# Three rooms for the summed weights, and a second room for g, in a block attention and squared-ReLU feed-forward kernel

## The chip, the cores and the metric

The kernel runs on one core of a Trainium2 chip. The metric is the device time of one execution in microseconds (us). The kernel before took 905.09 us (median of 3 runs, 904.5 to 905.71). One further execution was profiled; it took 905.52 us, of which 903.5 us lie between its first and its last instruction (the span). All rows below are from that execution.

## The reference

q, k and v have shape (8, 8, 576, 64): batch, heads, sequence, head width. Attention runs inside chunks of 64 positions only. The result is laid out as 4608 tokens of width 512 and goes through a feed-forward layer with a squared ReLU.

```python
scores = scale * np.matmul(q_c, k_c.transpose(0, 1, 2, 4, 3))   # chunks of 64
scores = scores - np.max(scores, axis=-1, keepdims=True)
attn = np.exp(scores)
attn = attn / (np.sum(attn, axis=-1, keepdims=True) + 1e-09)
out = np.matmul(attn, v_c)
...
h = x @ w_in            # 512 -> 2048, weights arrive as float64
r = np.maximum(h, 0.0)
g = r * r
return (g @ w_out).astype(np.float32)
```

## The kernel before

**Tiling.** The tokens are 36 pairs of chunks (128 tokens each), in 7 blocks: three of 4 pairs, four of 6. The hidden width 2048 is 16 slices of 128. Every float32 operand of the large products is split in a high and a low part, and each product takes three matmuls (high·high, high·low, low·high).

**Direct passes.** The first three blocks run slice by slice: 12 matmuls into h (L604), ReLU, square and split on ScalarE and VectorE, and two slices later 12 matmuls into the accumulators o (L640). These are 48 slices.

**Mixed blocks.** The last four blocks compute h with one level of a fast 2×2 scheme: 7 block products instead of 8. A *unit* (class Mixed) is one pair of hidden slices of one block: 7 products of 6 matmuls (L691) from mixed weights (the ring, 10 rooms, fetched from a scratch tensor in DRAM by L681) and mixed tokens (xc, made by build, L1225 and L1227). There are 8 units a block, 32 in all. Products accumulate in two PSUM banks, A (side 0) and C (side 1). Between products, ScalarE takes copies (keep, L697) and VectorE adds (add, L700) into float32 rooms: kept(0) for the first slice of the pair (gf0), kept(1) for the second (gf1). Then both are squared (L706) and split (high L709 on ScalarE, low L713 on VectorE): slice 0 into gs_s, slice 1 into gs_f. The second matrix product of a unit (L723, 6 groups with gs_f, then 6 with gs_s) stands behind the 7 products of the next unit. The third product needs bank A's copy, the fourth restarts bank C and so needs the unit's first add.

**Weight sums.** Four of the seven mixed weights of a slice pair are sums (s1 to s4). mix_weights makes them in three temp rooms on VectorE (L754 to L771). put then casts one (L774, ScalarE), subtracts for the low part (L778, VectorE) into the tile combo, and stores it to DRAM (L781, issued by GpSimd); a cast waits until the store before it has left combo. The other three weights are copied as they are (L790). There are 8 slice pairs, so 32 puts. They run beside the direct passes; the slots of wi12 to wi15 are taken over by xc and gs_f of the mixed blocks.

**Attention.** The pairs from 8 on (class Quad) run in clumps of 64 small matmuls on TensorE (L345 for the pair before, L298 for this one), with tiles e and p in two rooms each.

**Order.** Plan lists every step with a cost, the tiles it reads and writes, and a rank (lower goes first). Plan.run walks through a time line of its own and so fixes the order of each engine's instructions. On the chip each engine takes its instructions in that order and waits for the data of each. A gate only bars a step from being placed before another in the plan; it is no wait on the chip.

Of the kernel before, what the change touches and what calls it, by code (L numbers as in the profile page):

```python
# [20 lines left out]
def kernel(  # L21
# [24 lines left out]
    P = 128  # L46
# [228 lines left out]
    class Quad:  # L275
# [29 lines left out]
                nc.vector.tensor_reduce(self.m[:, c], four[c][:, 0], axis=AX.X, op=ALU.max)  # L305

        def less(self):
            self.e = late["pool"].tile([P, HH, 2, CH], F32, name=f"e{self.pair}", tag="e")
            for c in range(2):
                nc.vector.tensor_tensor(  # L310
                    self.e[:, :, c], four[c][:, 0], self.m[:, c].broadcast_to([P, HH, CH]), op=ALU.subtract
                )
# [17 lines left out]
            )  # L330

        def keep_p(self):
            self.p = late["pool"].tile([P, HH, 2, 2, CH // 2], F32, name=f"p{self.pair}", tag="p")
            nc.scalar.copy(self.p, self.et)

        def move_p(self, b, m):
# [199 lines left out]
        at = 2 * NCC * HN + i * HN  # L536
        return aside()[:, at:at + HN]

    def kept(i):

        return room(("g", i), lambda: gp.tile([P, 2 * HN], F32, name=f"gf{i}", tag=f"g{i + 1}", bufs=1))

    def in_slot(f, name, shape):
# [128 lines left out]
    class Mixed(Step):  # L672
# [3 lines left out]
        def __init__(self, b, p):  # L676
            self.b, self.p = b, p
            self.m = ((b - NCB) * NFP + p) * len(WAYS)

        def fetch(self, i):  # L680
            nc.gpsimd.dma_start(  # L681
# [15 lines left out]
            nc.scalar.copy(snap(i), sides[side][:, :HN])  # L697

        def add(self, i, h, side, s):
            nc.vector.tensor_tensor(kept(i)[:, h * HN:(h + 1) * HN], sides[side][:, :HN], snap(s), op=ALU.add)  # L700

        def positive(self):
            nc.scalar.activation(kept(1)[:, :HN], sides[0][:, :HN], AF.Relu)  # L703

        def square(self, i):
            nc.vector.scalar_tensor_tensor(kept(i), kept(i), 0.0, kept(i), op0=ALU.max, op1=ALU.mult)  # L706

        def high(self, i):
            nc.scalar.copy(split_g(i)[0], kept(i))  # L709

        def low(self, i):
            h, l = split_g(i)
            nc.vector.tensor_tensor(l, kept(i), h.bitcast(F32), op=ALU.subtract)  # L713

        def mm_out(self, i, j, u):
            b, p = self.b, self.p
# [14 lines left out]
    class Combos:  # L731
# [6 lines left out]
        def temp(self, i, n=1):  # L738
            return room("temp", lambda: gp.tile([P, 3, QW], F32, name="temp", tag="g2", bufs=1))[:, i:i + n]

        def out(self):
            return room("combo", lambda: wst.tile([P, 2, QW], F32R, name="combo", tag=f"a{VBUFS}"))

        def half(self, q):
# [25 lines left out]
            nc.vector.tensor_tensor(t, h, t, op=ALU.subtract)  # L770
            nc.vector.tensor_tensor(t, t, l, op=ALU.add)  # L771

        def high(self, i):
            nc.scalar.copy(self.out()[:, 0], self.temp(i)[:, 0])  # L774

        def low(self, i):
            o = self.out()
            nc.vector.tensor_tensor(o[:, 1], self.temp(i)[:, 0], o[:, 0].bitcast(F32), op=ALU.subtract)  # L778

        def store(self, name):  # L780
            nc.gpsimd.dma_start(  # L781
                out=combos[self.p, side_of[name]], in_=self.out().rearrange("p l n -> p (l n)")
            )

        def plain(self, q):
# [158 lines left out]
    def program():  # L944
# [165 lines left out]
        def scores(pair, gate):  # L1110
            x = quads[pair]
            i = pair % 2
            add(PE, 0.6, x.scores, ["qt", "kt"], ["sc", "A0", "C0"] + [("at", n) for n in range(2) if pair == NN],
                slack=SLACK, gate=gate)
            add(DVE, TWO, x.top, ["sc"], [("m", i)])
            add(DVE, TWO, x.less, ["sc", ("m", i)], [("e", i)])
            add(ACT, ONE, x.exps, [], [("e", i)])
            add(DVE, TWO + TINY, x.sums, [("e", i)], [("z", i)])
            add(DVE, TWO, x.norm, [("z", i)], [("e", i)])
            add(DVE, 0.73, x.turn_p, [("e", i)], ["et"])  # L1120
            add(ACT, ONE, x.keep_p, ["et"], [("p", i)] + [("p", i, *y) for y in itertools.product(range(2), repeat=2)])
            for b, m in itertools.product(range(2), repeat=2):
                add(SP, ISSUE, lambda b=b, m=m: x.move_p(b, m), ["et"], [("p", i, b, m)], size=P * DM // 2)

        def values(pair, gate):
            x = quads[pair]
            add(PE, 0.6, x.values, [("a", pair % VBUFS), ("p", pair % 2)] + [("p", pair % 2, *y) for y in itertools.product(range(2), repeat=2)], ["xt", "A1", "C1"], slack=SLACK, gate=gate)
# [52 lines left out]
        def wide(k):  # L1180

            return [("wh", item["i", k]), ("wl", item["i", k])]

        def mix_weights(c, gate):
            fs = [y for f in (2 * c.p, 2 * c.p + 1) for y in wide(f)]
            for q in ("a11", "a12", "a22"):
                add(POOL, 1.0, lambda q=q: c.plain(q), fs, [("combo", c.p, side_of[q])], size=P * DM * 4, gate=gate)
            T = [("temp", i) for i in range(3)]

            def put(i, name):  # L1190
                add(ACT, 0.4, lambda: c.high(i), [T[i]], ["ch"] + [("a", VBUFS)])
                add(DVE, 0.42, lambda: c.low(i), [T[i], "ch"], ["cl"])
                add(POOL, 1.0, lambda: c.store(name), ["ch", "cl"], [("combo", c.p, side_of[name])], size=P * DM * 4)

            add(DVE, 0.69, lambda: c.both_of(0, "21", "22", ALU.add), fs, T[:2], gate=gate)
            add(DVE, 0.42, lambda: c.join(0), [T[1]], [T[0]])
# [57 lines left out]
        def mixed(s, n):  # L1254
            first = s.m == 0
            rank, p.rank = p.rank, -20
            temp = [("temp", i) for i in range(3)] if first else []
            A, C = ["A0", "A1"], ["C0", "C1"]
            if n == 0:
                add(ACT, 0.5, lambda: s.keep(0, 0), A, ["s0"])  # L1260
            elif n == 1:
                add(DVE, 0.56, lambda: s.add(0, 0, 1, 0), C + ["s0"], [("kept", 0, 0)] + (["g"] if first else []))
            elif n == 2:
                add(ACT, 0.5, lambda: s.keep(1, 0), A, ["s1"])
            elif n == 3:
                add(ACT, 0.5, lambda: s.keep(0, 1), C, ["s0"])
            elif n == 4:
                add(DVE, 0.56, lambda: s.add(1, 1, 0, 0), A + ["s0"], [("kept", 1, 1)] + temp)
            elif n == 5:
                add(DVE, 0.56, lambda: s.add(0, 1, 1, 1), C + ["s1"], [("kept", 0, 1)])  # L1270
            elif n == 6:
                add(ACT, 0.5, lambda: s.positive(), A, [("kept", 1, 0)] + temp)
                square_of(s, 1)
                square_of(s, 0)
            p.rank = rank

        def square_of(s, i):
            p.rank = -1
            add(DVE, 0.95, lambda: s.square(i), [], [("kept", i, h) for h in range(2)])
            ends_to_come.append((s, i))  # L1280
            finish()

        ends_to_come = []

# [5 lines left out]
                parts_of(s, i)  # L1290
                p.rank = rank

        def parts_of(s, i):
            first = s.m == 0
            g = [("kept", i, h) for h in range(2)]
            for m, e, fn, cost in ((0, ACT, s.high, 0.82), (1, DVE, s.low, 0.95)):
                old = []
                if first:
                    old = wide(NF - 2) + wide(NF - 1) if i else [("g" + y, n) for y in "hl" for n in range(2)]
                add(e, cost, lambda fn=fn: fn(i), g + [("sg", i, 0)] * m, [("sg", i, m)] + old)  # L1300

        def mixed_group(s, i, j):
            n = item["o", 2 * s.p + i]
# [23 lines left out]
            else:  # L1327
                when.append(ends - NF + 0.3 + j * (NF - 1.3) / (SB - 1))
        mixers = [Combos(c) for c in range(NFP)]
        mix_at = [NF + 2 + (ends - NF - 9) * c / NFP for c in range(NFP)]  # L1330
        n = NF

        def clump(k, gate):
# [27 lines left out]
        for b in range(NCB, len(blocks)):  # L1361
            for c in range(NFP):
                s = Mixed(b, c)
                p.rank = 100
                fetch_ring(s)
                if c == 0:
                    p.rank = -1
                    build(b == NCB)
                p.rank = LASTS

# [6 lines left out]
                if c == 0 and b > NCB:  # L1377
                    outs(6)
                for i, more in enumerate((0, 4 if s.m == 0 else 0, 0, 0, 0, 0, 0)):
                    product(s, i)  # L1380
                    mixed(s, i)
                    if more:
                        outs(more)
                if 1 <= c <= SB and b < len(blocks) - 1:
                    at = outs(3)
                    clump(k, at)
# [2 lines left out]
                if some:  # L1389
                    outs(len(some))  # L1390
                some = [
                    (lambda s=s, i=i, j=j: mixed_group(s, i, j), i) for i in (1, 0) for j in range(blocks[b])
                ]
        outs(len(some))
        p.run()

# [33 lines left out]
```

## Time and profile before

| | |
|---|---|
| median of 3 runs | 905.09 us |
| profiled execution | 905.52 us |
| its span | 903.5 us |
| TensorE busy | 852.5 us, 94% of the span |
| VectorE, ScalarE, GpSimd busy | 548.3, 369.4, 242.4 us |
| direct passes end, mixed blocks begin | 320.15 us |
| second unit begins | 367.02 us |

TensorE is busy almost throughout. What is to be read is where in the span it is not, and what it waits for there. A row of the timeline gives the start, the duration, the engine, the line and tile, the number of instructions merged, and in brackets the idle time before it with what ended that.

### The profile page before, as it was taken

The page shows a single profiled execution, that of the slowest core. Times are in us where ns is not written, and L with a number is a line of the kernel's source. Part 1 is how long each engine was busy: PE and PEld are TensorE (multiplying, and loading weights), DVE is VectorE, ACT ScalarE, POOL GpSimd, SP SyncE. Part 2 cuts the span into 40 slices and gives each one's busy share as a digit, 9 for nine tenths or more (in the row PEclk, how much of TensorE's full clock was granted, in tenths as well). Part 3 has the DMA queues.
Part 4 walks back from the last instruction along what each step waited for, and adds up shares of the span by engine and source line. Part 5 has one row for each costly group of instructions (what it writes and reads, how often), then busy time and mean ns, then how long its engine had stood idle before and what let it go on. Part 6 is the DMA issues. An engine that isn't in the chain of part 4 may idle for free.

```text
span 903.5 us, 16529 instructions
## 1 busy us (share of the span) xinstructions
PE 852.5 (94%) x6142; PEld 732.0 (81%) x6142; DVE 548.3 (61%) x962; ACT 369.4 (41%) x669; POOL 242.4 (27%) x432
## 2 busy tenths in 40 slices
PE   9999999999999943999999999999999999999998
PEld 7787778888878832888888988888988888989896
DVE  6999994754755674555567565558555556533333
ACT  5898874444444431332224333225333324322221
POOL 2000022433551222333321423331332321313100
PEclk9999999999999976899999999999999999999999
DMA  8884525765984343567664866765766653644411
GB/s 203 256 260 135 200 48 131 155 140 119 251 172 102 90 111 99 167 148 171 157 140 101 239 141 155 167 154 116 219 151 136 149 135 82 202 113 125 121 46 70
DMA packets 241503, 132.72 MB, mean 147 GB/s; under 512 B 185744, under 2 KB 200336, under 8 KB 241424
## 3 DMA queue, kind: packets, MB, share of 16 engines
q0 software_dynamic: 47360, 80.77, 33.1%
q1 hardware_dynamic: 191808, 50.24, 25.1%
q8 instruction: 49, 0.80, 0.4%
q10 hardware_dynamic: 2256, 0.66, 0.3%
q14 instruction: 30, 0.25, 0.1%
HBM read 103.81 MB, written 24.12 MB: 142 GB/s over the span
## 4 chain that ended last, share of the span: by engine, by line
PE 79%; DVE 8%; issue 4%; DMA 3%; ACT 2%; SPq 2%; POOL 1%; DVEq 0%; POOLq 0%; ACTq 0%
PE o L723 30%; PE side L691 22%; PE o L640 12%; PE h L604 12%; PE side L345 2%; DVE gs_s L713 2%; PE side L298 2%; ACT gs_s L709 1%; SPq L260 1%; DVE gf L700 1%; ACT aside L697 1%; DMA k_raw<-in_k_dram 1%; DMA woraw<-in_moe_w_out_dram 1%; DVE woa L175 1%; DVE wia L175 1%
## 5 line engine op out<-in xcount | busy, mean ns | idle before, releaser
L691 PE MATMUL side<-xc,ring 128*128 128x384 f32 x1344 | 248.7, 340 | 42.6 <-DVE gf L700 29.5
L691 PEld LDWEIGHTS side<-xc,ring 128*128 128x128 f32 x1344 | 237.5, 190 | 51.7 <-DVE gf L700 19.8
L681 POOL DMA_DIRECT2D ring<-combos x224 | 121.5, 543 | 331.5 <-PE side L691 327.8
L604 PE MATMUL h<-x,wi 128*128 128x512 f32 x576 | 145.5, 395 | 1.6 <-ACT wi L187 1.0
L640 PE MATMUL o<-wo,gs 128*128 128x512 f32 x576 | 142.8, 395 | 0.0
L723 PE MATMUL o<-wo,gs_f 128*128 128x512 f32 x576 | 142.3, 395 | 0.0
L723 PE MATMUL o<-wo,gs_s 128*128 128x512 f32 x576 | 135.9, 389 | 0.0
L604 PEld LDWEIGHTS h<-x,wi 128*128 128x128 f32 x576 | 106.0, 188 | 26.5 <-DVE wi L197 2.7
L640 PEld LDWEIGHTS o<-wo,gs 128*128 128x128 f32 x576 | 108.9, 190 | 22.7
L723 PEld LDWEIGHTS o<-wo,gs_s 128*128 128x128 f32 x576 | 108.1, 188 | 22.3
L723 PEld LDWEIGHTS o<-wo,gs_f 128*128 128x128 f32 x576 | 106.4, 188 | 21.5
L700 DVE TENSOR_TENSOR gf<-side,aside 128x384 f32<-128x384 f32 x96 | 53.5, 558 | 103.7 <-PE side L691 101.5
L272 POOL DMA_DIRECT2D v_raw<-in_v_dram x112 | 69.8, 636 | 93.6 <-PE side L345 68.9
L697 ACT COPY aside<-side 128x384 f32<-128x384 f32 x96 | 46.0, 479 | 93.8 <-PE side L691 93.4
L713 DVE TENSOR_TENSOR gs_s<-gf,gs_s 128x768 fp32r<-128x768 f32 x32 | 30.6, 957 | 64.5 <-ACT gs_s L709 64.5
L630 DVE TENSOR_TENSOR gs<-g,gs 128x512 fp32r<-128x512 f32 x48 | 32.8, 683 | 52.1 <-ACT gs L627 52.1
L706 DVE SCALAR_TENSOR_TENSOR gf<-gf 128x768 f32<-128x768 f32 x64 | 61.0, 957 | 5.1 <-ACT gf L703 3.3
L703 ACT ACTIVATE gf<-side 128x384 f32<-128x384 f32 x32 | 15.7, 492 | 78.4 <-PE side L691 78.4
L713 DVE TENSOR_TENSOR gs_f<-gf,gs_f 128x768 fp32r<-128x768 f32 x32 | 30.0, 936 | 28.0 <-ACT gs_f L709 28.0
L305 DVE TENSOR_REDUCE m<-side 128x4 f32<-128x256 f32 x56 | 21.1, 419 | 39.9 <-ACT aside L357 36.9
L615 ACT ACTIVATE g<-h 128x512 f32<-128x512 f32 x48 | 28.5, 594 | 41.1 <-PE h L604 37.9
L627 ACT CAST gs<-g 128x512 fp32r<-128x512 f32 x48 | 29.8, 620 | 36.8 <-PE o L640 36.5
(110 smaller groups left out, 833.2 us busy)
## 6 DMA issues: line engine op xcount, KB each, us to landing
ring<-combos POOLq DMA_DIRECT2D x224, 256.0 KB, 3.4
wiraw<-in_moe_w_in_dram SPq DMA_DIRECT2D x16, 512.0 KB, 5.9
woraw<-in_moe_w_out_dram SPq DMA_DIRECT2D x16, 512.0 KB, 5.7
combos<-combo POOLq DMA_DIRECT2D x32, 256.0 KB, 2.5
out_dram<-ob SPq DMA_DIRECT2D x30, 256.0 KB, 3.0
q_raw<-in_q_dram SPq DMA_DIRECT2D x224, 32.0 KB, 2.2
k_raw<-in_k_dram SPq DMA_DIRECT2D x224, 32.0 KB, 2.9
v_raw<-in_v_dram POOLq DMA_DIRECT2D x112, 64.0 KB, 2.3
```

Of the source, the lines that this page charges most:

```text
L272: nc.gpsimd.dma_start(out=t[r, c], in_=s.rearrange("h j d -> j h d"))
L604: nc.tensor.matmul(self.h[:, :self.n], a[:, c], bb[:, c, :self.n], start=c == 0 and i == 0, stop=last,)
L627: nc.scalar.copy(self.gh[:, :self.n], self.g)
L630: nc.vector.tensor_tensor(self.gl[:, :self.n], self.g, self.gh.bitcast(F32)[:, :self.n], op=ALU.subtract)
L640: nc.tensor.matmul(acc[b, j], a[:, j * P:(j + 1) * P], bb, start=f == 0 and i == 0, stop=f == NF - 1 and i == 2,)
L681: nc.gpsimd.dma_start(out=ring(self.m + i).rearrange("p l c n -> p (l c n)"), in_=combos[self.p, i])
L691: nc.tensor.matmul(sides[side][:, :HN], w[:, l, c], part(x, r)[:, c], skip_group_check=True, start=(c, u) == (0, 0) and i in (0, 1, 3), st ...
L697: nc.scalar.copy(snap(i), sides[side][:, :HN])
L700: nc.vector.tensor_tensor(kept(i)[:, h * HN:(h + 1) * HN], sides[side][:, :HN], snap(s), op=ALU.add)
L706: nc.vector.scalar_tensor_tensor(kept(i), kept(i), 0.0, kept(i), op0=ALU.max, op1=ALU.mult)
L713: nc.vector.tensor_tensor(l, kept(i), h.bitcast(F32), op=ALU.subtract)
L723: nc.tensor.matmul(acc[b, j], a[:, j * P:(j + 1) * P], bb, start=first and u == 0, stop=last and u == 2)
```

## The change

combos gets three rooms: the old one and two in a new tile, taken in turn by the 32 puts, and the weight sums are planned one slice sooner and closer together. kept(0) gets a second room, gf2, for every other unit. The split of slice 0 (gs_s) is no longer added when the groups that read the old gs_s have been listed, but behind the seven products of the next unit. To make space, e and p of the attention get one room instead of two; the two new combo rooms and gf2 share one place (tag extra).

```diff
-            self.e = late["pool"].tile([P, HH, 2, CH], F32, name=f"e{self.pair}", tag="e")
+            self.e = late["pool"].tile([P, HH, 2, CH], F32, name=f"e{self.pair}", tag="e", bufs=1)
...
-    def kept(i):
-
+    def kept(i, n=0):
+
+        if n:
+            return room(("g", 2), lambda: late["pool"].tile([P, 2 * HN], F32, name="gf2", tag="extra", bufs=1))
...
+            self.turns = [p % 2, 0]
...
-        def out(self):
+        def out(self, b):
+            if b:
+                t = room("combos", lambda: late["pool"].tile([P, 2, 2, QW], F32R, name="combos", tag="extra", bufs=1))
+                return t[:, b - 1]
             return room("combo", lambda: wst.tile([P, 2, QW], F32R, name="combo", tag=f"a{VBUFS}"))
...
             def put(i, name):
-                add(ACT, 0.4, lambda: c.high(i), [T[i]], ["ch"] + [("a", VBUFS)])
-                add(DVE, 0.42, lambda: c.low(i), [T[i], "ch"], ["cl"])
-                add(POOL, 1.0, lambda: c.store(name), ["ch", "cl"], [("combo", c.p, side_of[name])], size=P * DM * 4)
+                b = next(turn_out) % 3
+                h, l = ("ch", b), ("cl", b)
+                add(ACT, 0.4, lambda: c.high(i, b), [T[i], "late"], [h] + [("a", VBUFS)] * (b == 0))
+                add(DVE, 0.42, lambda: c.low(i, b), [T[i], h], [l])
+                add(POOL, 1.0, lambda: c.store(name, b), [h, l], [("combo", c.p, side_of[name])], size=P * DM * 4)
...
         def square_of(s, i):
             p.rank = -1
-            add(DVE, 0.95, lambda: s.square(i), [], [("kept", i, h) for h in range(2)])
-            ends_to_come.append((s, i))
-            finish()
+            add(DVE, 0.95, lambda: s.square(i), [], [("kept", i, s.turns[i], h) for h in range(2)])
+            if i:
+                ends_to_come.append((s, i))
+                finish()
...
-        mix_at = [NF + 2 + (ends - NF - 9) * c / NFP for c in range(NFP)]
+        mix_at = [NF + 1 + (ends - NF - 10) * c / NFP for c in range(NFP)]
...
                 if c == 0:
-                    p.rank = -1
+                    if b > NCB:
+                        parts_of(before, 0)
                     build(b == NCB)
...
-                    product(s, i)
+                    at = product(s, i)
                     mixed(s, i)
                     if more:
                         outs(more)
+                if c:
+                    p.rank = -1
+                    parts_of(before, 0, at)
+                    p.rank = LASTS
+                before = s
```

VectorE in the first unit, before: behind the last transposes of the attention (kt19) stand sums of weights and their low parts, with the low parts of xc and the adds into gf between and behind them. This is the piece around xc7, up to the second add into gf0.

```order
L778 TENSOR_TENSOR combo_1854<-temp_1837,combo_1854 128x256
L754 TENSOR_TENSOR temp_1837<-wi12_1444,wi13_1524 128x512
L1227 TENSOR_TENSOR xc7_3860<-aside_2749,xc6_3795 128x768
L1227 TENSOR_TENSOR xc_3864<-aside_2749,xc8_3862 128x768
L757 TENSOR_TENSOR temp_1837<-temp_1837 128x256
L1227 TENSOR_TENSOR xc_3864<-aside_2749,xc_3864 128x768
L778 TENSOR_TENSOR combo_1854<-temp_1837,combo_1854 128x256
L754 TENSOR_TENSOR temp_1837<-wi15_1657 128x512
L700 TENSOR_TENSOR gf0_3800<-side1_81,aside_2749 128x384
```

VectorE in the first unit, after, from the low part of the last direct slice (gs2_15) to the unit's last two adds:

```order
L632 TENSOR_TENSOR gs2_15_3827<-g2_15_3799,gs2_15_3827 128x512
L324 TENSOR_TENSOR e18_3790<-e18_3790,z18_3811 128x512
L706 TENSOR_TENSOR gf0_3844<-side1_81,aside_2814 128x384
L1240 TENSOR_TENSOR xc7_3847<-aside_2814,xc6_3839 128x768
L1240 TENSOR_TENSOR xc_3855<-aside_2814,xc8_3815 128x768
L1245 TENSOR_TENSOR aside_2814<-aside_2814 128x768
L328 STREAM_TRANSPOSE et18_3868<-e18_3790 128x512
L1240 TENSOR_TENSOR xc_3855<-aside_2814,xc_3855 128x768
L290 STREAM_TRANSPOSE qt19_3881<-q_raw19_3620 128x512
L290 STREAM_TRANSPOSE kt19_3892<-k_raw19_3685 128x512
L706 TENSOR_TENSOR gf1_3902<-side0_80,aside_2814 128x384
L706 TENSOR_TENSOR gf0_3844<-side1_81,aside_2814 128x384
```

No sum of weights is left in this unit: the last low part of a sum now stands beside slice 6 of the third direct pass on VectorE. The transposes of pair 19 stand behind three low parts of xc; the last low part of xc follows the last row shown.

VectorE between a clump (pair 21's) and the squares of the unit behind it, before, from a split of gf1 to two of the unit's three adds:

```order
L713 TENSOR_TENSOR gs_f1_3952<-gf1_3926,gs_f0_3951 128x768
L324 TENSOR_TENSOR e21_4453<-e21_4453,z21_4471 128x512
L328 STREAM_TRANSPOSE et21_4490<-e21_4453 128x512
L713 TENSOR_TENSOR gs_s1_3968<-gf0_3800,gs_s0_3967 128x768
L700 TENSOR_TENSOR gf0_3800<-side1_81,aside_2749 128x384
L700 TENSOR_TENSOR gf1_3926<-side0_80,aside_2749 128x384
```

The same place after, down to the two squares:

```order
L719 TENSOR_TENSOR gs_f1_3943<-gf1_3902,gs_f0_3942 128x768
L324 TENSOR_TENSOR e21_4455<-e21_4455,z21_4473 128x512
L328 STREAM_TRANSPOSE et21_4492<-e21_4455 128x512
L706 TENSOR_TENSOR gf0_3844<-side1_81,aside_2814 128x384
L706 TENSOR_TENSOR gf1_3902<-side0_80,aside_2814 128x384
L706 TENSOR_TENSOR gf0_3844<-side1_81,aside_2814 128x384
L719 TENSOR_TENSOR gs_s1_4004<-gf2_3979,gs_s0_4003 128x768
L712 SCALAR_TENSOR_TENSOR gf0_3844<-gf0_3844 128x768
L712 SCALAR_TENSOR_TENSOR gf1_3902<-gf1_3902 128x768
```

The low part gs_s1 moved from ahead of the unit's three adds to behind them, ahead of the two squares; it reads gf2 while the adds write gf0.

## Rows read from the trace of the kernel before

**Rows 1.** Waits of TensorE: total us, number, longest.
```profile
PE side L691 <- DVE gf L700: 29.5, 17, 15.2
PE side L691 <- DVE xc L1227: 13.0, 2, 12.5
```

**Rows 2.** Timeline of TensorE around the first unit: start, us, line, tile, count, idle before.
```profile
307.95 2.88 PE L604 MATMUL h<-x,wi 128*128 128x512 f32 x12
...
322.26 2.92 PE L640 MATMUL o<-wo,gs 128*128 128x512 f32 x12
325.02 0.33 PE L691 MATMUL side<-xc,ring 128*128 128x384 f32 x1
337.83 5.63 PE L691 MATMUL side<-xc,ring 128*128 128x384 f32 x18 [12.48 <-DVE xc L1227]
...
360.37 2.26 PE L691 MATMUL side<-xc,ring 128*128 128x384 f32 x6 [15.19 <-DVE gf L700]
362.43 4.76 PE L640 MATMUL o<-wo,gs 128*128 128x512 f32 x12
367.02 7.47 PE L691 MATMUL side<-xc,ring 128*128 128x384 f32 x42
```

**Rows 3.** Windows: busy us (and count) of PE, PEld, DVE, ACT, POOL; clock, DMA share, GB/s.
```profile
130.00:325.00 195.00, 195.00 (x1443) 159.75 (x1442) 118.65 (x245) 91.31 (x174) 74.36 (x132) 1.00 0.62 142
325.00:337.00 12.00, 0.35 (x2) 0.00 (x0) 6.10 (x14) 2.01 (x5) 1.60 (x3) 0.66 0.50 100
...
458.00:462.00 4.00, 2.75 (x16) 2.44 (x15) 1.52 (x2) 0.99 (x3) 1.10 (x2) 1.00 0.99 209
```

**Rows 4.** Timeline of ScalarE: a ReLU of a direct slice, and two of the last sums.
```profile
305.43 0.60 ACT L615 ACTIVATE g<-h 128x512 f32<-128x512 f32 x1 [0.87 <-PE h L604]
...
355.25 0.40 ACT L774 CAST combo<-temp 128x256 fp32r<-128x256 f32 x1 [3.11 <-DMA combos<-combo]
358.77 0.40 ACT L774 CAST combo<-temp 128x256 fp32r<-128x256 f32 x1 [3.12 <-DMA combos<-combo]
```

**Rows 5.** The tile combo: the landing of its 32 stores.
```profile
DMA to landing us min/median/max: 2.2/2.5/5.1
```

**Rows 6.** Timeline of VectorE, first unit.
```profile
321.56 0.69 DVE L630 TENSOR_TENSOR gs<-g,gs 128x512 fp32r<-128x512 f32 x1
...
324.45 0.70 DVE L290 STREAM_TRANSPOSE qt<-q_raw 128x512 f32<-128x512 f32 x1
...
336.82 1.83 DVE L1227 TENSOR_TENSOR xc<-aside,xc 128x768 fp32r<-128x768 f32 x2
...
359.66 0.56 DVE L700 TENSOR_TENSOR gf<-side,aside 128x384 f32<-128x384 f32 x1
```

**Rows 7.** Timeline of VectorE, a unit with a clump.
```profile
386.36 0.96 DVE L713 TENSOR_TENSOR gs_s<-gf,gs_s 128x768 fp32r<-128x768 f32 x1 [2.23 <-ACT gs_s L709]
387.42 0.56 DVE L700 TENSOR_TENSOR gf<-side,aside 128x384 f32<-128x384 f32 x1
...
392.06 1.96 DVE L706 SCALAR_TENSOR_TENSOR gf<-gf 128x768 f32<-128x768 f32 x2
396.11 0.76 DVE L305 TENSOR_REDUCE m<-side 128x4 f32<-128x256 f32 x2 [2.10 <-ACT aside L357]
```

**Rows 8.** Timeline of TensorE: two of the 16 units in which it waits.
```profile
388.04 4.46 PE L691 MATMUL side<-xc,ring 128*128 128x384 f32 x24 [0.87 <-DVE gf L700]
...
460.40 4.49 PE L691 MATMUL side<-xc,ring 128*128 128x384 f32 x24 [1.25 <-DVE gf L700]
```

**Rows 9.** The chain that ended last: a whole unit of the last block, start, us.
```profile
782.09 7.34 PE side L691 x42
789.43 8.20 PE o L723 x36
```

**Rows 10.** Waits of GpSimd and ScalarE: total us, number, longest.
```profile
POOL v_raw L272 <- PE side L345: 68.9, 26, 8.2
...
ACT combo L774 <- DMA combos<-combo: 16.6, 5, 3.5
```

More of the change, by code (lines that the diff above doesn't have):

```diff
@@ L332, in keep_p @@
         def keep_p(self):
-            self.p = late["pool"].tile([P, HH, 2, 2, CH // 2], F32, name=f"p{self.pair}", tag="p")
+            self.p = late["pool"].tile([P, HH, 2, 2, CH // 2], F32, name=f"p{self.pair}", tag="p", bufs=1)
             nc.scalar.copy(self.p, self.et)
@@ L678, in __init__, with kept @@
             self.m = ((b - NCB) * NFP + p) * len(WAYS)
+            self.turns = [p % 2, 0]
+        def kept(self, i):
+            return kept(i, self.turns[i])
         def fetch(self, i):
@@ L699, in add @@
         def add(self, i, h, side, s):
-            nc.vector.tensor_tensor(kept(i)[:, h * HN:(h + 1) * HN], sides[side][:, :HN], snap(s), op=ALU.add)
+            nc.vector.tensor_tensor(self.kept(i)[:, h * HN:(h + 1) * HN], sides[side][:, :HN], snap(s), op=ALU.add)
         def positive(self):
-            nc.scalar.activation(kept(1)[:, :HN], sides[0][:, :HN], AF.Relu)
+            nc.scalar.activation(self.kept(1)[:, :HN], sides[0][:, :HN], AF.Relu)
         def square(self, i):
-            nc.vector.scalar_tensor_tensor(kept(i), kept(i), 0.0, kept(i), op0=ALU.max, op1=ALU.mult)
+            nc.vector.scalar_tensor_tensor(self.kept(i), self.kept(i), 0.0, self.kept(i), op0=ALU.max, op1=ALU.mult)
         def high(self, i):
-            nc.scalar.copy(split_g(i)[0], kept(i))
+            nc.scalar.copy(split_g(i)[0], self.kept(i))
         def low(self, i):
             h, l = split_g(i)
-            nc.vector.tensor_tensor(l, kept(i), h.bitcast(F32), op=ALU.subtract)
+            nc.vector.tensor_tensor(l, self.kept(i), h.bitcast(F32), op=ALU.subtract)
         def mm_out(self, i, j, u):
@@ L771, in from_it, with high, low, store @@
             nc.vector.tensor_tensor(t, t, l, op=ALU.add)
[L773 to L777, printed above, removed]
+        def high(self, i, b):
+            nc.scalar.copy(self.out(b)[:, 0], self.temp(i)[:, 0])
+        def low(self, i, b):
+            o = self.out(b)
             nc.vector.tensor_tensor(o[:, 1], self.temp(i)[:, 0], o[:, 0].bitcast(F32), op=ALU.subtract)
-        def store(self, name):
+        def store(self, name, b):
             nc.gpsimd.dma_start(
-                out=combos[self.p, side_of[name]], in_=self.out().rearrange("p l n -> p (l n)")
+                out=combos[self.p, side_of[name]], in_=self.out(b).rearrange("p l n -> p (l n)")
             )
@@ L1115, in scores @@
             add(DVE, TWO, x.top, ["sc"], [("m", i)])
[L1116 to L1121, printed above, removed]
+            add(DVE, TWO, x.less, ["sc", ("m", i)], [("e", 0)])
+            add(ACT, ONE, x.exps, [], [("e", 0)])
+            add(DVE, TWO + TINY, x.sums, [("e", 0)], [("z", i)])
+            add(DVE, TWO, x.norm, [("z", i)], [("e", 0)])
+            add(DVE, 0.73, x.turn_p, [("e", 0)], ["et"])
+            add(ACT, ONE, x.keep_p, ["et"], [("p", 0)] + [("p", 0, *y) for y in itertools.product(range(2), repeat=2)])
             for b, m in itertools.product(range(2), repeat=2):
-                add(SP, ISSUE, lambda b=b, m=m: x.move_p(b, m), ["et"], [("p", i, b, m)], size=P * DM // 2)
+                add(SP, ISSUE, lambda b=b, m=m: x.move_p(b, m), ["et"], [("p", 0, b, m)], size=P * DM // 2)
         def values(pair, gate):
             x = quads[pair]
-            add(PE, 0.6, x.values, [("a", pair % VBUFS), ("p", pair % 2)] + [("p", pair % 2, *y) for y in itertools.product(range(2), repeat=2)], ["xt", "A1", "C1"], slack=SLACK, gate=gate)
+            add(PE, 0.6, x.values, [("a", pair % VBUFS), ("p", 0)] + [("p", 0, *y) for y in itertools.product(range(2), repeat=2)], ["xt", "A1", "C1"], slack=SLACK, gate=gate)
             if x.b >= NCB:
@@ L1182, in wide @@
             return [("wh", item["i", k]), ("wl", item["i", k])]
+        turn_out = itertools.count()
         def mix_weights(c, gate):
@@ L1257, in mixed @@
             temp = [("temp", i) for i in range(3)] if first else []
+            k0 = ("kept", 0, s.turns[0])
+            extra = [(x, i) for x in ("ch", "cl") for i in (1, 2)] if s.m == len(WAYS) else ["g"] if first else []
             A, C = ["A0", "A1"], ["C0", "C1"]
@@ L1261, in mixed @@
             elif n == 1:
-                add(DVE, 0.56, lambda: s.add(0, 0, 1, 0), C + ["s0"], [("kept", 0, 0)] + (["g"] if first else []))
+                add(DVE, 0.56, lambda: s.add(0, 0, 1, 0), C + ["s0"], [k0 + (0,)] + extra)
             elif n == 2:
@@ L1267, in mixed @@
             elif n == 4:
-                add(DVE, 0.56, lambda: s.add(1, 1, 0, 0), A + ["s0"], [("kept", 1, 1)] + temp)
+                add(DVE, 0.56, lambda: s.add(1, 1, 0, 0), A + ["s0"], [("kept", 1, 0, 1)] + temp)
             elif n == 5:
-                add(DVE, 0.56, lambda: s.add(0, 1, 1, 1), C + ["s1"], [("kept", 0, 1)])
+                add(DVE, 0.56, lambda: s.add(0, 1, 1, 1), C + ["s1"], [k0 + (1,)])
             elif n == 6:
-                add(ACT, 0.5, lambda: s.positive(), A, [("kept", 1, 0)] + temp)
+                add(ACT, 0.5, lambda: s.positive(), A, [("kept", 1, 0, 0)] + temp)
                 square_of(s, 1)
@@ L1291, in finish, with parts_of @@
                 p.rank = rank
-        def parts_of(s, i):
+        def parts_of(s, i, gate=None):
             first = s.m == 0
-            g = [("kept", i, h) for h in range(2)]
+            g = [("kept", i, s.turns[i], h) for h in range(2)]
             for m, e, fn, cost in ((0, ACT, s.high, 0.82), (1, DVE, s.low, 0.95)):
@@ L1299, in parts_of @@
                     old = wide(NF - 2) + wide(NF - 1) if i else [("g" + y, n) for y in "hl" for n in range(2)]
-                add(e, cost, lambda fn=fn: fn(i), g + [("sg", i, 0)] * m, [("sg", i, m)] + old)
+                add(e, cost, lambda fn=fn: fn(i), g + [("sg", i, 0)] * m, [("sg", i, m)] + old, gate=gate)
         def mixed_group(s, i, j):
@@ L1383, in program @@
                         outs(more)
+                if c:
+                    p.rank = -1
+                    parts_of(before, 0, at)
+                    p.rank = LASTS
+                before = s
                 if 1 <= c <= SB and b < len(blocks) - 1:
@@ L1393, in program @@
                 ]
+        p.rank = -1
+        parts_of(before, 0)
+        p.rank = LASTS
         outs(len(some))
```

## The prediction, made before the changed kernel was run

> **What bounds the kernel now.** I read the granted clock and the shares first, then the waits of TensorE, then its timeline where the waits lie, then VectorE and ScalarE at those places. TensorE is busy for 852.5 of 903.5 us, so the question is only where it stands still. It has two waits that matter, both ahead of the block products (L691): 29.5 us in 17 pieces for an add into gf, and 13.0 us in 2 pieces for a low part of xc [rows 1]. The timeline parts these 42.5 us in two [rows 2, 8].
>
> First, one place: the first mixed unit. TensorE issues one matmul of the third product at 325.02, waits 12.48 us for xc, and later 15.19 us for the add; the second unit begins only at 367.02 [rows 2]. In that stretch the clock falls as well: 0.66 of full speed over 325 to 337 us [rows 3], and the 12 matmuls that took 2.92 us at 322.26 take 4.76 us at 362.43 [rows 2]. Why is the add late? VectorE and ScalarE are not full there: VectorE is busy for 6.1 of 12 us [rows 3]. They stand in line behind sums of weights. Each cast (L774) waits 3.1 us for the store before it to leave the one room, and two casts stand 358.77 - 355.25 = 3.52 us apart [rows 4]. The low parts of xc and the adds stand between these sums on VectorE's queue and get their turn at 336.82 and 359.66 [rows 6]. So a chain of DMA round trips, not arithmetic, sets the end of this stretch.
>
> Second, 16 units with a wait of about 0.87 us before the fourth product, one of them 1.25 [rows 8]; together 29.5 - 15.19 = 14.3 us [rows 1, 2]. The reader sees the cause in the two rows ahead of it on VectorE: the low part of gs_s runs from 386.36 for 0.96 us, and the add that TensorE needs follows at 387.42 [rows 7]; TensorE goes on at 388.04.
>
> Everywhere else TensorE is the bound: from 130 to 325 us it is busy for 195.00 of 195.00 us at full clock [rows 3], and units of the last block follow each other without a gap, 7.34 + 8.20 us [rows 9].
>
> **The change, part by part.**
>
> *Weight sums.* The sums are the same in number and size: 32 casts, low parts and stores, nothing added. With three rooms a cast waits for the store three puts earlier, and by the new order the last of them stands beside slice 6 of the third direct pass, some nine slices ahead of the first unit. So the whole stretch from 325.02 to 367.02, 42.0 us, is to be worked out anew. The work of TensorE in it is 30 matmuls of products and 12 of the last direct slice: 30 x 7.34 / 42 = 5.2 us [rows 9], and 325.02 - 322.26 = 2.8 us for the 12 [rows 2], 8.0 us at full clock. What is late next is VectorE. Its new order behind the low part at 321.56 [rows 6] is: normalisation, add, two xc, one minus, a transpose, one xc, two transposes, add, add, xc. I step by start to start, which for rows back to back is some 0.09 us less than the duration (two xc in 1.83 us, so 0.87 each; the transposes 0.61; the adds 0.48) [rows 6]: 0.61 + 0.61 + 0.48 puts the first xc at 323.3 and its end at 324.2, before TensorE comes to the third product at 325.02; five more 0.87 and 0.61 steps in that order put the second xc's end at 325.1, well ahead of the fifth product (327.1), and the third's at 327.5, ahead of the sixth (328.2). The two transposes keep VectorE until 328.7, so the add behind the fifth product ends at 329.2, when the sixth product ends as well. The add behind the sixth ends near 330.0, and the last low part of xc at 330.9: the seventh product has issued one matmul at 329.3 and waits about 1.5 us for it. The stretch becomes 8.0 + 1.5 = 9.5 us; 42.0 - 9.5 = 32.5 us gained. Bounds of that wait: 0, if VectorE keeps ahead, and about 3 us, if the two transposes find their data late. I take 1.5, as worked out.
>
> Does the clock fall in this wait? The nearest row is a wait of 1.25 us, with the clock at 1.00 over 458 to 462 us [rows 8, 3]; I take full clock. The Trainium skill (TensorE: Matmul & The Clock Gate, Part 1) says that the array's default is the half clock and that only activity keeps it at 2.4 GHz. By that rule the wait could cost the clock too; no wait of this length in the trace shows it. If it did, the 12 matmuls behind would take 4.76 instead of 2.92 us [rows 2], 1.8 us more; that is inside my range.
>
> What hides the sums in their new place? In the direct passes VectorE is busy for 118.65 and ScalarE for 91.31 of 195 us [rows 3]; the eleven puts that move add 11 x (0.40 us on ScalarE and a like time on VectorE), so there is room in the mean. The tight point is the one bank h: a ReLU ended at 306.03 and the next slice's h began at 307.95 [rows 2, 4], so ScalarE may be 1.9 us late. It would be if a cast stood ahead of a ReLU waiting for its room. Below nothing: TensorE has no wait there to give back. Above: five casts have waited 16.6 us in all, 3.5 at most [rows 10]; 5 x (3.5 - 1.9) = 8 us. I take 0: a room's round takes 3.5 us [rows 4], or with the slowest landing instead of the usual one 3.5 - 2.5 + 5.1 = 6.1 us [rows 4, 5], and three rooms in turn give a put every 2.0 us; the 32 puts now have some 22 slices of 5.4 us, one every 3.7 us. Without that cover (a store held behind a v_raw that waits up to 8.2 us on GpSimd's queue [rows 10]) the 8 us come back.
>
> *The second room of g.* The low part of gs_s goes from ahead of the three adds to behind them, and nothing is added: 32 splits before and after. The add is then first in line, and all 16 waits go: -14.3 us. What the split delays are the two squares, by 0.96 us; they ran from 392.06 to 394.0, and the next work of VectorE waits until 396.11 [rows 7], so 2.1 us lie open. What reads the split are the second six groups of the unit before; they stand behind seven products and six groups, 7.34 + 4.1 us from the unit's start [rows 9], and the low part ends about 8.0 us after it (add behind the sixth product at 6.5, 0.5 for it, 0.96 for the split). 3.4 us are left over, more with a clump. Bounds: 0 to 14.3 us gained; I take all, since no other row stands between the product and its add. At block changes the split stays where the old gs_s comes free, and TensorE shows no wait there in either order's place: 0.
>
> *One room for e and p.* e is written and last read on VectorE's own queue, in that order; p's reader stands ahead of the next pair's scores in the same clump. No wait is possible that the order does not hold already: 0.
>
> **Sum.** 903.5 - 32.5 - 14.3 = 856.7 us of span. The profiled execution's time is 2.0 us above its span and 0.4 us above the median: 856.7 + 2.0 = 858.7 against its 905.5, and 858.3 against the median. One unit has its copy of p 0.7 us later by the new order and may stop TensorE for 0.3: 858.6.
>
> **Rivals.**
> (1) The sums collide in the direct passes or the unit is slower than worked out: ReLUs late by the 8 us above, the first unit's wait 3 us instead of 1.5, or a few tenths left in the 16 units (the odd 0.38 in [rows 8] times 16 is 6 us). For it: GpSimd's queue holds v_raw loads that wait [rows 10], and the DMA engines are busy for 0.62 there [rows 3]. Against it: TensorE lost nothing there with one room. Time: 862 to 875, say 867. The Trainium skill (DMA: Bandwidth & Descriptors, "Issuing engines are not separate DMA queues") says that DMAs of all issuing engines share the same 16 DMA engines and interleave; by that rule stores packed closer stretch each other. The landing of 2.5 us with 5.1 at most agrees with some of that [rows 5]; by the rule alone the sum stays, since even 5.1 is covered, but it is why this case has the chance that it has.
> (2) Only one part comes. The first unit then waits for something the sums hid, such as ring transfers: half of 32.5 is lost, 875; or the waits of the 16 units stay: 873. Against: the ring's rooms of the second unit come free at the same point of the first as before, 12 us ahead of their use.
> (3) The changed order does not take effect on the chip, because the sums are still late: 904. Against: the order shows no sum in the first unit.
> (4) Slower: the split, once behind the products, comes too late for its six groups. If it lands behind the attention's work on VectorE rather than ahead of the squares, TensorE waits ahead of gs_s in each of some 28 units. It pays from 3.4 us of delay on and loses all of the gain (46.8 us) at 3.4 + 46.8 / 28 = 5.1 us; at 6 us it is 858.6 + 28 x 2.6 = 931. Against: by the order it stands ahead of the squares.
>
> **How the numbers follow.** Forecast 0.78, (1) 0.14, (2) 0.05, (3) 0.01, (4) 0.02. What a measurement of this kernel can tell from no change is about 0.2%, 1.8 us. All cases but (3) and (4) are faster by far: faster 0.97, same 0.01, slower 0.02. Predicted: 858.6 us. The range of the forecast reaches from 855.5 (no wait in the first unit, and a small gain that I do not see) to 863; to leave out no more than two in ten it takes in most of (1): 855 to 868.
>
> **What would show it.** Right: the second unit starts near 334.5 us; TensorE's wait for xc in the first unit is 1 to 2 us and that for the add is gone; the clock stays at 1.00 from 320 to 345 us; no cast waits for a store for more than a microsecond in the direct passes; the 16 rows of 0.87 us are gone, and units with a clump come every 16.8 to 17.0 us. Wrong: a new row of waits ahead of h (L604 before), ahead of o<-gs_s, or of the ring.

## The result, and the profile after

The changed kernel takes 855.37 us (median of 4 runs, 855.31 to 856.38) against 905.3 us before in the same comparison: ratio 0.9452, 95% interval 0.9436 to 0.9469, 49.9 us less. The forecast was 858.6 us, with 855 to 868 as its range. The profiled execution took 856.38 us, 1.0 us more than the three others; it is late from the start (TensorE's first wait for a converted weight ends at 36.91 us before and at 38.06 here). That is no part of the change: in the other profiled executions below it ends anywhere from 37.34 to 38.10 us, at 38.09 in a kernel with the old sums and the old g.

The lines have moved: the block products are L697 (old L691), the direct slice's output products L642 (L640), the adds L706 (L700), the squares L712 (L706) and the low parts of the splits L719 (L713). The waits of TensorE, block products only, answer to [rows 1]:

```profile
PE side L697 <- DVE xc L1240: 1.3, 1, 1.3
```

42.5 us in 19 pieces have become 1.3 us in one. The timeline of TensorE around the first unit answers to [rows 2]:

```profile
321.75 2.27 PE L697 MATMUL side<-xc,ring 128*128 128x384 f32 x12
323.86 2.92 PE L642 MATMUL o<-wo,gs 128*128 128x512 f32 x12
326.62 4.58 PE L697 MATMUL side<-xc,ring 128*128 128x384 f32 x25
332.49 1.16 PE L697 MATMUL side<-xc,ring 128*128 128x384 f32 x5 [1.29 <-DVE xc L1240]
333.49 2.92 PE L642 MATMUL o<-wo,gs 128*128 128x512 f32 x12
336.25 7.49 PE L697 MATMUL side<-xc,ring 128*128 128x384 f32 x42
...
353.09 7.51 PE L697 MATMUL side<-xc,ring 128*128 128x384 f32 x42
```

From the third product (326.62) to the second unit (336.25) it is 9.63 us instead of 42.0. Without the later arrival at the unit (1.60 us, table below) the second unit begins at 334.65, where 334.5 was forecast. The one wait left is the seventh product's, after its first matmul: it stands where 25 matmuls end and 5 are left. The 12 matmuls behind it take 2.92 us again. The window from 318 to 335 us shows the granted clock (1.00) and how full VectorE is (15.65 of 17 us):

```profile
318.00:335.00 17.00, 15.71 (x79) 13.90 (x78) 15.65 (x25) 8.87 (x15) 5.06 (x10) 1.00 0.54 124
```

On VectorE the second unit answers to [rows 7]: the three adds, then the split, then the squares, and 1.47 us open ahead of the attention's next work.

```profile
341.74 0.56 DVE L706 TENSOR_TENSOR gf<-side,aside 128x384 f32<-128x384 f32 x1 [2.58 <-PE side L697]
342.71 0.56 DVE L706 TENSOR_TENSOR gf<-side,aside 128x384 f32<-128x384 f32 x1 [0.42 <-PE side L697]
343.19 0.95 DVE L719 TENSOR_TENSOR gs_s<-gf,gs_s 128x768 fp32r<-128x768 f32 x1
344.06 1.82 DVE L712 SCALAR_TENSOR_TENSOR gf<-gf 128x768 f32<-128x768 f32 x2
347.35 0.76 DVE L305 TENSOR_REDUCE m<-side 128x4 f32<-128x256 f32 x2 [1.47 <-ACT aside L357]
```

The waits around the sums answer to [rows 10]: GpSimd's loads of values wait longer, and only one cast waits for a store.

```profile
POOL v_raw L272 <- PE side L345: 80.5, 23, 15.2
...
ACT combo L783 <- DMA combos<-combo: 0.9, 1, 0.9
```

The stores have become slower to land (the 11 from the old room; [rows 5] showed 2.5 in the median and 5.1 at most):

```profile
DMA to landing us min/median/max: 2.4/3.2/7.2
```

The span in three stretches, from the starts of the first product and of the second unit (ends against starts, in us):

| | before | after | difference |
|---|---|---|---|
| up to the first product | 320.15 | 321.75 | +1.60, of it 1.15 by 38 us |
| first unit (to the second's start) | 46.87 | 14.50 | -32.37 |
| second unit to the end | 536.48 | 518.35 | -18.13 |
| span | 903.5 | 854.6 | -48.9 |

### The profile page after: what moved, and what is told of

It is laid out like the page before. It is cut to its first block, busy times and chain, and to the rows that moved or that the text cites. A ratio compares the mean times of both kernels' runs of the same rounds, so it can differ in the third digit from the quotient of the medians.

```text
span 854.6 us, 16517 instructions
## 1 busy us (share of the span) xinstructions
PE 845.0 (99%) x6142; PEld 729.6 (85%) x6142; DVE 540.6 (63%) x962; ACT 367.8 (43%) x669; POOL 242.5 (28%) x432
## 4 chain that ended last, share of the span: by engine, by line
PE 88%; DVE 10%; issue 1%; POOL 0%; ACT 0%; POOLq 0%; DVEq 0%
PE o L729 31%; PE side L697 28%; PE o L642 12%; PE h L606 11%; PE side L345 2%; PE side L298 2%; DVE wia L175 1%; DVE woa L175 1%; DVE wi L197 1%; DVE wia L182 1%; DVE woa L182 1%; DVE wo L197 1%; DVE wia L163 1%; DVE wia L169 1%; DVE gs L632 1%
## 5 line engine op out<-in xcount | busy, mean ns | idle before, releaser
L697 PE MATMUL side<-xc,ring 128*128 128x384 f32 x1344 | 241.3, 336 | 1.3 <-DVE xc L1240 1.3
L697 PEld LDWEIGHTS side<-xc,ring 128*128 128x128 f32 x1344 | 235.7, 188 | 4.9 <-DVE xc L1240 1.5
L706 DVE TENSOR_TENSOR gf<-side,aside 128x384 f32<-128x384 f32 x96 | 53.5, 557 | 170.6 <-PE side L697 166.6
L642 PE MATMUL o<-wo,gs 128*128 128x512 f32 x576 | 141.7, 392 | 0.0
L642 PEld LDWEIGHTS o<-wo,gs 128*128 128x128 f32 x576 | 107.2, 188 | 22.3
L712 DVE SCALAR_TENSOR_TENSOR gf<-gf 128x768 f32<-128x768 f32 x64 | 58.6, 952 | 1.1 <-ACT gf L709 0.9
L719 DVE TENSOR_TENSOR gs_f<-gf,gs_f 128x768 fp32r<-128x768 f32 x32 | 30.0, 937 | 23.7 <-ACT gs_f L715 23.7
L334 ACT COPY p<-et 128x512 f32<-128x512 f32 x28 | 17.4, 622 | 52.2 <-DVE et L328 51.9
```

The costliest lines, as they stand in the source:

```text
L642: nc.tensor.matmul(acc[b, j], a[:, j * P:(j + 1) * P], bb, start=f == 0 and i == 0, stop=f == NF - 1 and i == 2,)
L697: nc.tensor.matmul(sides[side][:, :HN], w[:, l, c], part(x, r)[:, c], skip_group_check=True, start=(c, u) == (0, 0) and i in (0, 1, 3), st ...
L706: nc.vector.tensor_tensor(self.kept(i)[:, h * HN:(h + 1) * HN], sides[side][:, :HN], snap(s), op=ALU.add)
L712: nc.vector.scalar_tensor_tensor(self.kept(i), self.kept(i), 0.0, self.kept(i), op0=ALU.max, op1=ALU.mult)
L719: nc.vector.tensor_tensor(l, self.kept(i), h.bitcast(F32), op=ALU.subtract)
```

## The experiments

All ran against the kernel before (905.08 us median in the comparisons of the first four runs below, 904.94 in that of the two kernels timed side by side, 904.91 in the others). The edits stand against the changed kernel, the last one against the kernel before.

**One part alone: the sums.**

```diff
-            self.turns = [p % 2, 0]
+            self.turns = [0, 0]
...
-            if i:
-                ends_to_come.append((s, i))
-                finish()
+            ends_to_come.append((s, i))
+            finish()
...
-                    parts_of(before, 0, at)
```

> Weight sums as in the changed kernel, kept(0) in one room and the split of slice 0 in its old place. Theory A (a wait costs what the start of the next matmul shows, 18.01 - 16.84 = 1.17 us a unit): the 16 waits of 0.87 us come back and cost 18 to 19 us, so 855.4 + 18.5 = 873.9 us. Rival (a wait costs its row, 14.3 us in all, and 2 us of the gain came from elsewhere): 869.7 us. In both the first unit takes the 9.6 us of the changed kernel at full clock.

872.87 us, ratio 0.9644 (0.9629 to 0.9658). That is 17.5 us above the changed kernel. TensorE's waits and one of the units in its timeline:

```profile
PE side L697 <- DVE gf L706: 13.1, 15, 0.9
...
PE side L697 <- DVE xc L1240: 1.3, 1, 1.3
```

```profile
369.24 3.31 PE L697 MATMUL side<-xc,ring 128*128 128x384 f32 x18
373.42 4.48 PE L697 MATMUL side<-xc,ring 128*128 128x384 f32 x24 [0.87 <-DVE gf L706]
377.74 2.24 PE L729 MATMUL o<-wo,gs_f 128*128 128x512 f32 x9
...
387.25 3.31 PE L697 MATMUL side<-xc,ring 128*128 128x384 f32 x18
```

The unit lasts 387.25 - 369.24 = 18.01 us against 353.09 - 336.25 = 16.84 us for the second unit of the changed kernel, without the wait: 1.17 us, of which the row shows 0.87. (The next units there last 16.87 us, which makes it 1.14.) Of the 16 waits 15 came back. Their rows add up to 13.1 us; the medians differ by 17.5 us, with 2.4 us between the fastest and the slowest run here, and the two traces from the second unit to the end by 870.5 - 335.50 - 518.35 = 16.65 us. So theory A holds: a wait costs more than its row. Its time, 873.9, was for 16 waits and is 1.0 us too high; the rival's, 869.7, is 3.2 us too low.

The rows show where the rest goes. The 18 matmuls are given 3.31 us, but back to back they start every 0.174 us (42 in 7.32), so the next would have started 3.14 us after the first; the rest of the row is the modelled end of the last matmul, which beside other matmuls is hidden. The idle time counts only from there. The next matmul started 4.18 us after the first, 1.04 late. The 24 behind it then take 377.74 - 373.42 = 4.32 us from start to start instead of 24 x 0.174 = 4.18, which is another 0.14.

**The other part alone: the room of g and the moved split.**

```diff
-                b = next(turn_out) % 3
+                b = next(turn_out) % 1
...
-        mix_at = [NF + 1 + (ends - NF - 10) * c / NFP for c in range(NFP)]
+        mix_at = [NF + 2 + (ends - NF - 9) * c / NFP for c in range(NFP)]
```

> One room for the sums and their old time; the second room of g and the moved split as in the changed kernel. Theory A (the two parts are independent): the first unit's stretch is 42 us again, the 16 waits are gone: 855.4 + 32.4 = 887.8 us. Rival (the parts share something, the moved split or gf2 helps the first unit as well or is hurt by the sums): off that by more than 2 us, with the first unit's stretch shorter or longer than 42 us.

885.7 us, ratio 0.9786 (0.9769 to 0.9802): 30.3 us above the changed kernel, 19.4 us below before. The 16 waits are gone and the first unit's two are back:

```profile
PE side L697 <- DVE gf L706: 15.2, 1, 15.2
PE side L697 <- DVE xc L1240: 12.4, 2, 12.1
```

```profile
325.45 0.33 PE L697 MATMUL side<-xc,ring 128*128 128x384 f32 x1
337.87 5.88 PE L697 MATMUL side<-xc,ring 128*128 128x384 f32 x18 [12.09 <-DVE xc L1240]
...
360.39 2.26 PE L697 MATMUL side<-xc,ring 128*128 128x384 f32 x6 [15.20 <-DVE gf L706]
362.45 3.55 PE L642 MATMUL o<-wo,gs 128*128 128x512 f32 x12
365.84 7.53 PE L697 MATMUL side<-xc,ring 128*128 128x384 f32 x42
```

The stretch lasts 365.84 - 325.45 = 40.4 us here, not 42.0: the waits are the same within 0.6 us, and the 12 matmuls take 3.55 instead of 4.76 us, at a granted clock of 0.73 from 360 to 367 us instead of 0.54. The time is 2.1 us below theory A's 887.8, and by its letter that, with the shorter stretch, is the rival. But this stretch is not the same from one execution to the next either: the kernel with one room for e and p (last run below) has the order of the kernel before on VectorE there, and its trace shows 367.42 - 326.16 = 41.26 us, with the 12 matmuls at 3.69 us. So at most about a microsecond is left for an effect of the split on the first unit, and whether there is one stays open. 32.2 us (905.08 - 872.87) for the sums and 19.4 for the split make 51.6, against 49.9 together; the difference of 1.7 us is about what this stretch lacks here (1.6). Within about 2 us the parts are independent.

**The room without the place.** The changed kernel with the split listed in its old place.

```diff
-            if i:
-                ends_to_come.append((s, i))
-                finish()
+            ends_to_come.append((s, i))
+            finish()
...
-                    parts_of(before, 0, at)
```

> The changed kernel with the second room of g, but the split of slice 0 listed in its old place. Theory A (what held the add back was the room: the add overwrites what the split still reads, so it had to queue behind it; with a room of its own the planner puts the first add ahead of the split by itself in all but two units with a clump): 855.4 + 2 x 1.2 = 857.8 us. Rival (the place behind the products is what counts, the room only makes it possible): the 16 waits stay, 873 us.

855.73 us, ratio 0.9456 (0.9442 to 0.947): the same as the changed kernel within 0.4 us. No wait for gf is left. VectorE in a unit with a clump shows what the planner makes of the free room:

```profile
372.58 0.56 DVE L706 TENSOR_TENSOR gf<-side,aside 128x384 f32<-128x384 f32 x1 [2.17 <-PE side L697]
373.05 0.95 DVE L719 TENSOR_TENSOR gs_s<-gf,gs_s 128x768 fp32r<-128x768 f32 x1
375.73 0.56 DVE L706 TENSOR_TENSOR gf<-side,aside 128x384 f32<-128x384 f32 x1 [1.73 <-PE side L697]
```

The planner has put the first add ahead of the split by itself. With one room it could not: the add overwrites what the split still reads. So theory A holds in its cause: the room is what counts, and the place behind the products adds nothing that can be measured. The two units with a clump in which the split still stands ahead showed no wait for gf either, so the 2.4 us that theory A put down for them did not come. In one of them the split ran at 353.36, early enough, but the copy of p came late and the clump waited 0.50 us for its transfer.

**Rooms without the earlier time.**

```diff
-        mix_at = [NF + 1 + (ends - NF - 10) * c / NFP for c in range(NFP)]
+        mix_at = [NF + 2 + (ends - NF - 9) * c / NFP for c in range(NFP)]
```

> The changed kernel with three rooms for the sums but the old planned times (one slice later, wider spacing). Theory A (the rooms do it: a cast no longer waits a whole store; no sum stands in the first unit by the order): 855.4 us, within 1 us. Rival (the slice is needed, the last sums come into the first unit on the chip): a wait for xc or an add of 3 to 15 us there, 859 to 870 us.

855.0 us, ratio 0.9448 (0.9434 to 0.9462). Theory A: with three rooms the earlier time is not needed. The last low part of a sum starts at 285.0 us, well ahead of the first unit, and that has the same wait, 1.30 us.

**The earlier time without rooms.**

```diff
-                b = next(turn_out) % 3
+                b = next(turn_out) % 1
```

> The changed kernel with one room for the sums, at the new earlier times. By the order five low parts of sums still stand ahead of the last two adds of the first unit. Theory A (each costs one round trip of the room, 3.5 us): the first unit waits about 15 to 17 us for an add, and the clock falls for the matmuls behind it, 855.4 + 16 + 2 = 873 us. Rival (VectorE's own work on the sums is what delays the add, about 1 us a sum): 860 us. Second rival (starting sooner is enough): 856 us.

874.85 us, ratio 0.9669 (0.9655 to 0.9682). ScalarE shows the five sums that are still left for the first unit:

```profile
332.91 0.40 ACT L783 CAST combo<-temp 128x256 fp32r<-128x256 f32 x1 [2.10 <-DVE temp L766]
336.81 0.40 ACT L783 CAST combo<-temp 128x256 fp32r<-128x256 f32 x1 [3.50 <-DMA combos<-combo]
340.59 0.40 ACT L783 CAST combo<-temp 128x256 fp32r<-128x256 f32 x1 [3.37 <-DMA combos<-combo]
344.11 0.41 ACT L783 CAST combo<-temp 128x256 fp32r<-128x256 f32 x1 [3.12 <-DMA combos<-combo]
347.62 0.40 ACT L783 CAST combo<-temp 128x256 fp32r<-128x256 f32 x1 [3.11 <-DMA combos<-combo]
```

```profile
349.22 2.26 PE L697 MATMUL side<-xc,ring 128*128 128x384 f32 x6 [19.08 <-DVE gf L706]
351.28 4.31 PE L642 MATMUL o<-wo,gs 128*128 128x512 f32 x12
```

They come 3.5 to 3.9 us apart, one store each, and TensorE waits 19.08 us. VectorE is busy for 9.32 of the 19 us from 330 to 349 there, so its arithmetic is not what holds the add. This is theory A with a slightly longer wait than its 15 to 17 us (873 us was expected). Beside the run with the split alone (885.7 us), which differs from this one only in the planned times, it also shows what the earlier time is worth with one room: 10.9 us, where with three rooms it was worth nothing.

**Two rooms.**

```diff
-                b = next(turn_out) % 3
+                b = next(turn_out) % 2
```

> The changed kernel with two rooms for the sums instead of three, at the new times. Theory A (a put every 3.7 us is needed and two rooms give one every 1.8 to 3 us): no sum in the first unit, 855.4 us within 1 us. Rival (the third room is needed because GpSimd's queue holds stores behind loads of values): casts wait for stores in the direct passes, ReLUs late, 857 to 865 us.

855.86 us, ratio 0.946 (0.9447 to 0.9473). Theory A: two rooms do as well. The casts waited for stores 1.2 us in all there, and the first unit's wait is 1.33 us.

**Two groups ahead of the seventh product.**

```diff
-                for i, more in enumerate((0, 4 if s.m == 0 else 0, 0, 0, 0, 0, 0)):
+                for i, more in enumerate((0, 4 if s.m == 0 else 0, 0, 0, 0, 2 if s.m == 0 else 0, 0)):
```

> The changed kernel with two of the last direct slice's four output groups placed ahead of the first unit's seventh product instead of behind it (1.36 us of other work for TensorE). Theory A (the last wait of the first unit, 1.29 us for a low part of xc, is VectorE's pace, and any work put ahead of it hides it; two groups are left behind the product to hide the ReLU of bank A): 855.4 - 1.4 = 854.0 us, no wait for xc. Rival (the wait moves on to the first product of the second unit, which restarts bank A): 855.4 us.

854.01 us, ratio 0.9437 (0.9424 to 0.945), 1.36 us below the changed kernel's median; the intervals of the two ratios overlap, so this comparison alone does not part the two. The trace shows what theory A expected:

```profile
326.58 4.35 PE L697 MATMUL side<-xc,ring 128*128 128x384 f32 x24
330.77 1.55 PE L642 MATMUL o<-wo,gs 128*128 128x512 f32 x6
332.16 1.43 PE L697 MATMUL side<-xc,ring 128*128 128x384 f32 x6
333.42 1.55 PE L642 MATMUL o<-wo,gs 128*128 128x512 f32 x6
334.81 7.45 PE L697 MATMUL side<-xc,ring 128*128 128x384 f32 x42
```

The wait is gone, nothing takes its place, and the stretch lasts 334.81 - 326.58 = 8.23 us. TensorE then has no wait for block products at all.

Both kernels were then timed side by side, the changed kernel once more and the version with two groups ahead:

> The changed kernel once more, on one chip with the next run, so that the two can be compared: 855.4 us within 0.7.

> The version with two of the last direct slice's output groups ahead of the seventh product, beside the changed kernel on one chip. Theory A (the whole of the first unit's last wait is gained, 9.63 - 8.23 us by the two traces): 1.4 us below the run before it. Rival (the difference of the first comparison was the chip's): within 0.5 us of it.

855.56 us (5 runs, 855.25 to 855.66) against 853.68 us (4 runs, 853.31 to 854.38): 1.9 us less, and every run of the second lies below every run of the first. The stretch accounts for 9.63 - 8.23 = 1.4 us of it, as theory A had it; the other 0.5 us stays open.

**One room for e and p, alone.**

```diff
-            self.e = late["pool"].tile([P, HH, 2, CH], F32, name=f"e{self.pair}", tag="e")
+            self.e = late["pool"].tile([P, HH, 2, CH], F32, name=f"e{self.pair}", tag="e", bufs=1)
...
-            self.p = late["pool"].tile([P, HH, 2, 2, CH // 2], F32, name=f"p{self.pair}", tag="p")
+            self.p = late["pool"].tile([P, HH, 2, 2, CH // 2], F32, name=f"p{self.pair}", tag="p", bufs=1)
```

> The kernel before with e and p of the attention in one room each and nothing else changed. Theory A (the order of the queues already holds them apart): 905.3 us within 0.5. Rival (the single rooms cost something in the clumps, so the changed kernel would gain more with two): 907 us or more.

904.57 us, ratio 0.9997 (0.9988 to 1.0006): no cost in the kernel before. It is theory A, though the time lies 0.7 us below its 905.3, and 0.3 below the kernel before of that comparison. In the changed kernel it was not tried by itself; there TensorE shows no wait for p.

## Why the prediction was right, and where its sizes were off

- **Weight sums, right in mechanism and size.** The stretch was worked out as 9.5 us with a wait of 1.5 us for the last low part of xc; it is 9.63 us with 1.29. Stepping VectorE's new order by start-to-start times was enough. The cause, one store's round trip for each cast, is shown by the run at the earlier times with one room. The prediction did not part the rooms from the earlier times; the runs do: rooms alone do it, and two suffice.
- **The second room of g: the term that was mis-sized.** "All 16 waits go: -14.3 us" took the idle rows for the cost. The waits went, but the stretch from the second unit on shrank by 18.13 us, 1.13 us for each of 16. That is 3.8 us more than the sum had, and more than the 3.2 us by which the result beats the forecast; the direct stretch, below, takes some of it back.
- **The range.** The time lies 0.4 us above the lower end of 855. That end stood for a first unit without its wait and a small gain not seen, and not for a gain of 18 us from g. That the result stayed inside is in part luck.
- **What the split would push back** was nothing: the squares end 1.47 us ahead of the attention's next work, where 2.1 us less 0.96 had been expected to be left. The 0.3 us put down for a late copy of p did not come.
- **The clock.** It stayed at 1.00 through the 1.29 us wait, as the row of 1.25 us had suggested. The case that the prediction took from the Trainium skill (TensorE: Matmul & The Clock Gate, Part 1), a clock that falls in this wait, did not arise. The runs with the long waits show what it costs: 12 matmuls at 3.55 to 4.76 us instead of 2.92.
- **Rival (1), the collision in the direct passes.** Its premise came in part: the stores landed later, 3.2 us in the median instead of 2.5 and 7.2 at most. With one room at the same planned times the median is 2.6, with two rooms 3.2, so it rose with the further rooms and not with the earlier time. That agrees with what the Trainium skill (DMA: Bandwidth & Descriptors, "Issuing engines are not separate DMA queues") says, that DMAs of all issuing engines run on the same 16 DMA engines and interleave. A load of values also waited up to 15.2 us on GpSimd's queue. But one cast waited, 0.9 us, and no ReLU was late enough for TensorE. What had been put at 0 there is 0.45 us beyond the late start, and it is no wait: the traces of all the runs with three rooms show it (283.6 to 283.7 us from the first wait for a weight to the first product of the first unit), those with one or two do not (283.2 to 283.3). Most of it stands at one place. Before, the two halves of an attention clump follow each other at 278.88 and 279.40, and 12 matmuls into h, the clump and 12 matmuls into o take 284.87 - 278.11 = 6.76 us. After, nine matmuls into h part the halves (280.10 and 282.99), and the same work takes 286.47 - 279.33 = 7.14 us.
- **Rivals (2) to (4)** did not occur.

## What to carry to other kernels

An engine that shows half its time idle can still be the one waited for: look in its queue for instructions that wait for a transfer's round trip, and give that transfer a second room before moving the work. Where an add overwrites what a slower step still reads, a second room lets the planner reorder the two by itself. And price a wait by the next start against the start it would have had, not by its idle row.

## What the runs showed of the hardware that was not expected

An idle row of TensorE of 0.87 us cost 1.13 to 1.17 us, since the modelled end of the last matmul (0.17 us) and a slower start behind the wait (0.14 us) come on top. After the waits of 12 and 15 us in the kernel before, the granted clock was 0.54 in the mean from 360 to 367 us, so at half (1.2 of 2.4 GHz) for most of the work there, and how long it stays so differed between two traces with the same order there: the same 12 matmuls took 4.76 us in the kernel before and 3.69 us in the one with a single room for e and p. The one attention clump cost 0.38 us more when nine of the large matmuls parted its halves than when they followed each other.
